# Top-k attention and MLP on one core: conversion by an integer add, division after the values product, loads in order of need

## The chip, the cores and the metric

The kernel runs on one core of a Trainium2 chip. Its engines work side by side, each on its own queue of instructions: TensorE (in the profile PE for matmuls and PEld for the loading of their stationary operands), VectorE (DVE), ScalarE (ACT), GpSimd (POOL) and SyncE (SP), which issues all DMAs here. The metric is the device time of one execution in microseconds (us); lower is better.

## The reference

Two blocks follow each other. The first is attention that keeps only the 32 largest scores of each row:

```python
scores = scale * np.matmul(q, k.transpose(0, 1, 3, 2))          # 8 x 8 heads, 576 x 576
kth = np.partition(scores, -top_k, axis=-1)[..., -top_k:-top_k + 1]
scores = np.where(scores >= kth, scores, -1000000000.0)
attn = np.exp(scores - np.max(scores, axis=-1, keepdims=True))
attn = attn / (np.sum(attn, axis=-1, keepdims=True) + 1e-09)
attn_out = np.matmul(attn, v)                                   # (8, 8, 576, 64)
```

The second is an MLP on its output, taken as 4608 tokens of 512 features:

```python
h = x @ w_in                                                    # 4608 x 2048
g = np.where(h >= 1, h, np.where(h <= -1, 0.0, (h + 1) ** 2 / 4))
out = g @ w_out                                                 # 4608 x 512
```

q, k and v are fp32. `w_in` and `w_out` come as 64-bit floats, so the kernel reads each number as two 32-bit words (`lo`, `hi`) and makes an fp32 number of them itself. Numbers that are nearly zero are set to zero (the comparison of `size` with 1.125 * 2^-15).

## The kernel before

Attention is cut into 144 steps. A step is one tile of 128 query rows for a pair of heads (`t < NT`), or, for the last 64 rows of a sequence, a tail tile that serves two pairs (`t == NT`). `steps` lists them in order: batch by batch, within a batch tile by tile, within a tile pair by pair.

Each step goes through these functions. `scores` (L209) multiplies queries and keys on TensorE into four PSUM tiles `sp` and copies them to `s` on ScalarE (L224). `weights` (L229) finds the 32nd largest value on VectorE: it takes the larger of each two scores (`more`, L238), then four rounds of `max` and three of `match_replace` (L244, L251), then the smaller ones (`less`, L256) to see whether a pair hid a large second score. ScalarE forms `exp` (L248) once GpSimd has the negated maximum (L246). VectorE masks `e` and sums it (L271), takes the reciprocal `rz` of the sum (L277), and GpSimd multiplies `e` by it (L279). `transpose_w` (L283) turns `e` on TensorE in eight transposes plus one for the 64 left-over columns of both heads, and ScalarE copies them to `wT` and `wTt` (L291, L294). `values` (L297) multiplies them by v into a PSUM tile `po`, which ScalarE copies to `xT` (L318, L320), the input of the MLP.

The MLP of a chunk of one or two tiles is a list of work items (`mlp`, L329): sixteen `hidden` (TensorE into `ph`, two activations on ScalarE, three operations on GpSimd, L343 to L345), then `final` items, two of the sixteen slices of `w_out` each, into `py`; the last copies `y` and stores it.

The loop of L445 sets the order. Iteration m issues, on TensorE, values(m-2), scores(m+1), some MLP items, transpose_w(m-1), the transposes of later queries and keys, more MLP items; on VectorE, weights(m). The order on TensorE and VectorE is that of the program (`manual_schedule`, L411); ScalarE, GpSimd and the DMA queue are ordered by a scheduler. How many MLP items an iteration takes is decided when the program is built: `share` is what is left divided by the iterations left, an item is taken when its cost is covered and the weights that it needs are `converted`, and unspent credit is capped at 8. Where a chunk is used up before the next is ready, iterations hold no MLP item. This happens around the iterations 14 to 16, 25, 26, 61, 62, 96 to 98, 106, 124 and 134 to 136.

All PSUM tiles of attention share one tag of four buffers (`tag="a", bufs=4`), handed out in turn: in iteration m `po` takes one, the four `sp` of scores(m+1) the next four, so the fourth needs the buffer of `po` back.

The weights are converted in 64 pieces of 128 x 256 numbers (`weight_piece`, L78). A piece takes three operations on VectorE (L85, L86, L90), two on ScalarE (L92, L97), two on GpSimd (L93, L94), and, one piece later, the mask on VectorE (L99). `convert` is called four times ahead of step 0 and six times in each `weights`, from the callback `between` (four rounds, after the masking, after the reciprocal), so the pieces are done in step 9.

After all steps the largest `excess` is turned into a flag (L475 to L483). If the shortcut with pairs was not enough, the whole is run again without it (L485).

Of the kernel before, what the change touches and what calls it, by code (L numbers as in the profile page):

```python
# [22 lines left out]
def kernel(  # L23
# [10 lines left out]
    nc = tc.nc  # L34
# [25 lines left out]
    nc.gpsimd.memset(minus, -1.0)  # L60
    w_in = const.tile([P, NK, DFF], F32, name="w_in")
# [16 lines left out]
    def weight_piece(pool, dst, src):  # L78
        raw = pool.tile([P, 2 * WC], U32, name="raw", bufs=2)
        nc.sync.dma_start(out=raw, in_=src.bitcast(U32))  # L80
        words = raw.rearrange("p (n t) -> p n t", t=2)
        lo, hi = words[:, :, 0], words[:, :, 1]

        top = pool.tile([P, WC], U32, name="top", bufs=2)
        nc.vector.tensor_scalar(top, hi, 3, 0x3FFFFFFF, ALU.logical_shift_left, ALU.bitwise_and)  # L85
        nc.vector.scalar_tensor_tensor(out=top, in0=hi, scalar=0xC0000000, in1=top,  # L86
                                       op0=ALU.bitwise_and, op1=ALU.bitwise_or)

        unit = pool.tile([P, WC], U32, name="unit", bufs=2)
        nc.vector.tensor_scalar(unit, top, 0xFF800000, None, ALU.bitwise_and)  # L90
        low = pool.tile([P, WC], F32, name="low", bufs=2)
        nc.scalar.activation(low, lo, AF.Copy, scale=2.0 ** -52)  # L92
        nc.gpsimd.tensor_tensor(out=low, in0=low, in1=unit.bitcast(F32), op=ALU.mult)  # L93
        nc.gpsimd.tensor_tensor(out=low, in0=low, in1=top.bitcast(F32), op=ALU.add)  # L94

        size = pool.tile([P, WC], F32, name="size", bufs=2)
        nc.scalar.activation(size, hi.bitcast(F32), AF.Abs)  # L97
        yield
        nc.vector.scalar_tensor_tensor(out=dst, in0=size, scalar=1.125 * 2.0 ** -15, in1=low,  # L99
                                       op0=ALU.is_ge, op1=ALU.mult)  # L100

    def weight_pieces(pool):

        pieces = [(w_in[:, kk, c:c + WC], moe_w_in[kk * P:(kk + 1) * P, c:c + WC])
                  for c in range(0, DFF, WC) for kk in range(NK)]
        pieces += [(w_out[:, f, c:c + WC], moe_w_out[f * P:(f + 1) * P, c:c + WC])
                   for f in range(NF) for c in range(0, DM, WC)]
        before = None
        for dst, src in pieces:
            piece = weight_piece(pool, dst, src)  # L110
# [11 lines left out]
    def run(ctx, paired):  # L122
# [47 lines left out]
        def keys_of(b):  # L170

            kT = stage.tile([P, NHP, S], F32, name="kT")
            v_in, v_tl = load_values(b)
            k_tl = stage.tile([TL, H, D], F32, name="k_tl", bufs=1)
            nc.sync.dma_start(out=k_tl, in_=k[b, :, SM:S, :].rearrange("h p d -> p h d"))
            for hp in range(NHP):
                k_in = stage.tile([P, NT, 2, D], F32, name="k_in")
                for j in range(2):
                    nc.sync.dma_start(out=k_in[:, :, j, :], in_=whole(k, b)[:, 2 * hp + j])
                pt = ps.tile([P, NT, P], F32, name="pk", tag="a", bufs=4)  # L180
# [13 lines left out]
                yield dict(kT=kT, v=v_in, v_tl=v_tl)  # L194
# [34 lines left out]
        def weights(st, between):  # L229
# [48 lines left out]
            for i in range(2):  # L278
                nc.gpsimd.tensor_scalar(e[:, i, :], e[:, i, :], rz[:, i:i + 1], 1.0, ALU.mult, ALU.mult)  # L279
# [3 lines left out]
        def transpose_w(st):  # L283
            w = st["e"]
            st["wT"] = wT = att.tile([P, 2, NT, P], F32, name="wT", bufs=1)
            st["wTt"] = wTt = att.tile([P, P], F32, name="wTt", bufs=1)
# [5 lines left out]
            pt = ps.tile([P, P], F32, name="pwt", tag="a", bufs=4)  # L292
            nc.tensor.transpose(pt, w.rearrange("p i n -> p (i n)")[:, SM:SM + P], ident)
            nc.scalar.copy(wTt, pt)  # L294


        def values(st):  # L297
            t, hp, v_in, v_tl = st["t"], st["hp"], st["keys"]["v"], st["keys"]["v_tl"]
            wT, wTt = st["wT"], st["wTt"]
            po = ps.tile([P, P], F32, name="po", tag="a", bufs=4)  # L300
            if t < NT:
                for c in range(NT + 1):
                    for j in range(2):
                        h = 2 * hp + j
                        nc.tensor.matmul(po[j * D:(j + 1) * D], v_in[:, h, c, :] if c < NT else v_tl[0][:, h, :],  # L305
                                         wT[:, j, c, :] if c < NT else wTt, start=(c == 0), stop=(c == NT))
            else:
                for i in range(2):
                    cols = slice(i * TL, (i + 1) * TL)
                    for c in range(NT + 1):  # L310
                        for j in range(2):
                            h = 2 * (hp + i) + j
                            nc.tensor.matmul(po[j * D:(j + 1) * D, cols], v_in[:, h, c, :] if c < NT else v_tl[1][:, h, :],
                                             wT[:, i, c, j * TL:(j + 1) * TL] if c < NT else wTt[:, j * TL:(j + 1) * TL],
# [106 lines left out]
        for got in keys_of(0):  # L421
            keys[0] = got
# [92 lines left out]
```

## Time and profile before

| | |
|---|---|
| median of 3 runs | 1918.03 us (1916.92 to 1918.96) |
| the profiled execution | 1915.05 us, span 1913.0 us |
| TensorE busy (PE) | 1679.1 us, 88% of the span |
| VectorE busy (DVE) | 1625.4 us, 85% |
| GpSimd busy (POOL) | 1028.8 us, 54% |
| ScalarE busy (ACT) | 977.1 us, 51% |
| mean granted TensorE clock | 0.942 |
| the chain that ended last | PE 53%, DVE 22%, POOL 13%, ACT 6%, issue 5%, DMA 1% |

The span runs from the first instruction to the last. "L244 x1152" is line 244 of the kernel, executed 1152 times; the tiles are written out<-in. In an answer on waits, "PE pw L290 <- POOL e L279" says that TensorE stood idle before the instruction of line 290 that writes `pw` until GpSimd finished the instruction of line 279 that writes `e`. In a timeline each row has its start and its length in us, the engine, the line, the operation, and in brackets the idle time ahead of it. An average over the whole span hides that the stages have different limits, so the stages have to be read one by one.

### The profile page before, as it was taken

To read this page: it belongs to the slowest core of one execution; us is meant where nothing else is said; L and a number is where in the kernel's file an instruction comes from. 1 tells how busy PE (TensorE), PEld (TensorE's weight loads), DVE (VectorE), ACT (ScalarE), POOL (GpSimd) and SP (SyncE) were. 2 spreads that over 40 slices of the span, in tenths; PEclk is the share of its full clock that TensorE was granted. 3 is DMA by queue.
4 is the path that set the end of the run, shared out by engine and by line. 5 is a ranking of instruction groups with operands and counts; after the bars stand their busy time and mean duration, and the time that the engine had idled before them with its cause. 6 is when DMAs were issued, how large, how long until landed. Compare 5 with 4: busy or idle time off the path is not lost.

```text
span 1913.0 us, 32251 instructions
## 1 busy us (share of the span) xinstructions
PE 1679.1 (88%) x10129; PEld 1160.1 (61%) x10129; DVE 1625.4 (85%) x5011; ACT 977.1 (51%) x2429; POOL 1028.8 (54%) x1772
## 2 busy tenths in 40 slices
PE   2346478898999999998999999998999999998998
PEld 1234255656676685767575776666676667666565
DVE  5998989999999799999898898989987879879640
ACT  4345455546455564655454655555455555445432
POOL 3567572725454672818283674637274554553553
PEclk8667679899999999999999999999999999998999
DMA  6222210011010000110010000110010000000000
GB/s 173 80 78 77 77 28 17 26 30 24 9 40 20 23 18 23 32 36 12 16 38 23 21 12 24 40 27 12 23 31 25 11 12 11 10 12 7 6 7 14
DMA packets 107445, 57.75 MB, mean 30 GB/s; under 512 B 86272, under 2 KB 94464, under 8 KB 107264
## 3 DMA queue, kind: packets, MB, share of 16 engines
q1 hardware_dynamic: 107264, 55.59, 10.6%
q8 instruction: 82, 1.34, 0.3%
q14 instruction: 99, 0.81, 0.1%
HBM read 46.14 MB, written 9.44 MB: 29 GB/s over the span
## 4 chain that ended last, share of the span: by engine, by line
PE 53%; DVE 22%; POOL 13%; ACT 6%; issue 5%; DMA 1%; POOLq 0%; SPq 0%; DVEq 0%; ACTq 0%
PE py L353 24%; PE ph L336 11%; PE sp L221 6%; DVE tops L244 6%; PE po L305 5%; DVE more L251 5%; PE pw L290 4%; POOL g L345 4%; POOL r L344 3%; POOL e L279 2%; POOL r L343 2%; DVE e L271 2%; DVE more L238 2%; DVE seconds L259 2%; DVE less L256 1%
## 5 line engine op out<-in xcount | busy, mean ns | idle before, releaser
L353 PE MATMUL py<-w_out,g 128*128 128x512 f32 x1152 | 534.7, 607 | 41.7 <-DVE w_out L99 37.1
L336 PE MATMUL ph<-xT,w_in 128*128 128x256 f32 (+1 forms) x2816 | 553.3, 353 | 3.9 <-ACT g L342 2.8
L336 PEld LDWEIGHTS ph<-xT,w_in 128*128 128x128 f32 x2816 | 466.4, 197 | 83.0 <-issue 29.4
L244 DVE MAX8 tops<-more 128x8 f32<-128x288 f32 x1152 | 468.5, 448 | 5.0
L353 PEld LDWEIGHTS py<-w_out,g 128*128 128x128 f32 x1152 | 209.2, 191 | 286.4 <-issue 219.8
L251 DVE MATCH_REPLACE8 more<-tops,more 128x288 f32<-128x288 f32 x864 | 375.9, 443 | 0.0
L279 POOL TENSOR_SCALAR e<-e,rz 128x576 f32<-128x576 f32 x288 | 242.4, 850 | 130.9 <-DVE rz L277 104.9
L340 ACT ACTIVATE r<-ph,half 128x256 f32<-128x256 f32 (+1 forms) x352 | 153.9, 437 | 264.2 <-POOL g L345 135.2
L264 POOL TENSOR_TENSOR excess<-seconds,kth 128x2 f32<-128x2 f32 x144 | 39.2, 273 | 417.3 <-DVE kth L263 416.4
L271 DVE SCALAR_TENSOR_TENSOR e<-s,kth,e 128x576 f32<-128x576 f32 x288 | 242.4, 875 | 23.1 <-ACT e L248 6.6
L345 POOL TENSOR_TENSOR g<-r,g 128x256 f32<-128x256 f32 (+1 forms) x352 | 246.7, 701 | 24.0
L291 ACT COPY wT<-pw 128x512 f32<-128x512 f32 x288 | 155.5, 594 | 202.3 <-PE pw L290 202.3
L290 PE MATMUL pw<-ident,e 128*128 128x128 f32 x1152 | 161.5, 284 | 110.6 <-POOL e L279 105.9
L248 ACT ACTIVATE e<-s,nmax 128x576 f32<-128x576 f32 x288 | 213.1, 786 | 75.2 <-POOL nmax L246 74.4
L238 DVE TENSOR_TENSOR more<-s 128x576 f32<-128x576 f32 x144 | 130.4, 905 | 139.0 <-ACT s L224 138.6
L344 POOL TENSOR_TENSOR r<-r 128x256 f32<-128x256 f32 (+1 forms) x352 | 230.4, 655 | 26.1
L290 PEld LDWEIGHTS pw<-ident,e 128*128 128x128 f32 x1152 | 138.0, 146 | 162.5 <-POOL e L279 118.2
L221 PE MATMUL sp<-kT,qT 64*128 64x288 f32 x1024 | 196.5, 442 | 34.7 <-ACT xT L318 26.4
L224 ACT ACTIVATE s<-sp 128x288 f32<-128x288 f32 x576 | 197.9, 417 | 40.7 <-PE sp L221 36.8
L343 POOL TENSOR_SCALAR r<-r 128x256 f32<-128x256 f32 (+1 forms) x352 | 155.4, 441 | 93.5 <-ACT r L340 93.2
L305 PEld LDWEIGHTS po<-wT,v_in 128*64 128x64 f32 x2048 | 118.0, 140 | 74.8 <-issue 40.0
L221 PEld LDWEIGHTS sp<-kT,qT 64*128 64x128 f32 x1024 | 109.1, 189 | 84.6 <-ACT xT L318 39.4
(61 smaller groups left out, 1592.7 us busy)
## 6 DMA issues: line engine op xcount, KB each, us to landing
q_in<-in_q_dram SPq DMA_DIRECT2D x32, 256.0 KB, 3.0
v_in<-in_v_dram SPq DMA_DIRECT2D x8, 1024.0 KB, 5.8
k_in<-in_k_dram SPq DMA_DIRECT2D x64, 128.0 KB, 3.0
raw<-in_moe_w_in_dram SPq DMA_DIRECT2D x32, 256.0 KB, 2.7
raw<-in_moe_w_out_dram SPq DMA_DIRECT2D x32, 256.0 KB, 2.8
out_dram<-y SPq DMA_DIRECT2D x32, 256.0 KB, 2.3
v_tail<-in_v_dram SPq DMA_DIRECT2D x16, 64.0 KB, 2.5
k_tl<-in_k_dram SPq DMA_DIRECT2D x8, 128.0 KB, 3.2
```

Of the source, the lines that this page charges most:

```text
L221: nc.tensor.matmul(o[:, a0 - c0:a1 - c0], qT[d, g, :], kT[d, g, k0:k0 + a1 - a0], start=True, stop=True)
L244: nc.vector.max(out=tops[:, i, r:r + 8], in_=src[:, i, :])
L248: nc.scalar.activation(e[:, i, :], s[:, i, :], AF.Exp, bias=nmax[:, i:i + 1])
L251: nc.vector.match_replace(out=rest[:, i, :], in_to_replace=tops[:, i, r:r + 8], in_values=src[:, i, :], imm_value=LOWEST)
L271: nc.vector.scalar_tensor_tensor(out=e[:, i, :], in0=s[:, i, :], scalar=last[:, i:i + 1], in1=e[:, i, :], op0=ALU.is_ge, op1=ALU.mult, acc ...
L279: nc.gpsimd.tensor_scalar(e[:, i, :], e[:, i, :], rz[:, i:i + 1], 1.0, ALU.mult, ALU.mult)
L290: nc.tensor.transpose(pt[:, c, :], w[:, i, main(i)][:, c * P:(c + 1) * P], ident)
L305: nc.tensor.matmul(po[j * D:(j + 1) * D], v_in[:, h, c, :] if c < NT else v_tl[0][:, h, :], wT[:, j, c, :] if c < NT else wTt, start=(c == ...
L336: nc.tensor.matmul(ph, w_in[:, kk, f * P:(f + 1) * P], xT[:, kk, 0:cw], start=(kk == 0), stop=(kk == NK - 1))
L344: nc.gpsimd.tensor_tensor(out=r, in0=r, in1=r, op=ALU.mult)
L345: nc.gpsimd.tensor_tensor(out=g[:, 0:cw], in0=r, in1=g[:, 0:cw], op=ALU.add)
L353: nc.tensor.matmul(py, gs[f][:, i * P:(i + 1) * P], w_out[:, f, :], start=(f == 0), stop=(f == NF - 1))
```

## The change

Five things change.

1. Loads. `keys_of` issues the keys of the first head pair first, then the 64-row remainder, and v after the second pair. For batch 0 only the first pair is prepared before step 0; the others follow after the first eight conversions. `raw` has three buffers where it had two.
2. Conversion. The low word becomes a number between 2 and 2 + 2^-19 (`units`). Its bits, added as an integer on GpSimd to the shifted high word, round the mantissa and mend the exponent in one operation. VectorE shifts (one operation) and later puts the sign in (one). For `w_in` the mask moves to GpSimd (a comparison and a product); for `w_out` it stays on VectorE.
3. Division. GpSimd no longer scales `e`. `rz` is spread by a ScalarE copy to `rzw`, transposed on TensorE behind the left-over columns (one transpose, two in a tail step), copied with `wTt`, and `divide` multiplies `po` by it on VectorE when it writes `xT` (two instructions in a tail step). `divide(m-2)` is run from the first `between` of weights(m), that is after the first round of step m.
4. MLP share. In iterations 0 to 11 the share is at least 52, and eight pieces are converted ahead of step 0.
5. Flag. `judge` runs in the last iteration with attention, right after weights(143), instead of after everything. `y` has one buffer where it had two.

The core of the diff:

```diff
-    def weight_piece(pool, dst, src):
-        raw = pool.tile([P, 2 * WC], U32, name="raw", bufs=2)
+    def weight_piece(pool, dst, src, mask_engine):
+        raw = pool.tile([P, 2 * WC], U32, name="raw", bufs=3)
...
-        nc.vector.tensor_scalar(top, hi, 3, 0x3FFFFFFF, ALU.logical_shift_left, ALU.bitwise_and)
-        nc.vector.scalar_tensor_tensor(out=top, in0=hi, scalar=0xC0000000, in1=top,
-                                       op0=ALU.bitwise_and, op1=ALU.bitwise_or)
...
-        nc.vector.tensor_scalar(unit, top, 0xFF800000, None, ALU.bitwise_and)
...
-        nc.gpsimd.tensor_tensor(out=low, in0=low, in1=unit.bitcast(F32), op=ALU.mult)
-        nc.gpsimd.tensor_tensor(out=low, in0=low, in1=top.bitcast(F32), op=ALU.add)
...
+        nc.scalar.activation(units, lo, AF.Identity, bias=two, scale=2.0 ** -51)
...
+        nc.vector.tensor_scalar(bits, hi, 3, None, ALU.logical_shift_left)
+        nc.gpsimd.tensor_tensor(out=bits.bitcast(I32), in0=bits.bitcast(I32), in1=units.bitcast(I32), op=ALU.add)
+        if mask_engine is nc.gpsimd:
+            nc.gpsimd.tensor_scalar(size, size, 1.125 * 2.0 ** -15, 1.0, ALU.is_ge, ALU.mult)
         yield
-        nc.vector.scalar_tensor_tensor(out=dst, in0=size, scalar=1.125 * 2.0 ** -15, in1=low,
-                                       op0=ALU.is_ge, op1=ALU.mult)
+        nc.vector.scalar_tensor_tensor(out=bits, in0=hi, scalar=0x80000000, in1=bits,
+                                       op0=ALU.bitwise_and, op1=ALU.bitwise_or)
+        if mask_engine is nc.gpsimd:
+            nc.gpsimd.tensor_tensor(out=dst, in0=size, in1=bits.bitcast(F32), op=ALU.mult)
+        else:
+            nc.vector.scalar_tensor_tensor(out=dst, in0=size, scalar=1.125 * 2.0 ** -15, in1=bits.bitcast(F32),
+                                           op0=ALU.is_ge, op1=ALU.mult)
...
-            for i in range(2):
-                nc.gpsimd.tensor_scalar(e[:, i, :], e[:, i, :], rz[:, i:i + 1], 1.0, ALU.mult, ALU.mult)
+            if st["t"] < NT:
+                st["rzw"] = rzw = att.tile([P, 2, D], F32, name="rzw")
+                nc.scalar.copy(rzw, rz.unsqueeze(2).broadcast_to([P, 2, D]))
...
+            if st["t"] < NT:
+                nc.tensor.transpose(pt[:, 1], rzw.rearrange("p i d -> p (i d)"), ident)
+                nc.scalar.copy(wTt[:, 0:2], pt[:, 0:2])
...
+        def divide(st):
...
-                nc.scalar.copy(xT[:, hp, col:col + P], po)
+                nc.vector.tensor_tensor(out=xT[:, hp, col:col + P], in0=po, in1=wTt[:, 1], op=ALU.mult)
...
-        for _ in range(4):
+        for _ in range(8 if paired else 0):
             convert()
...
+            def between():
+                if todo:
+                    todo.pop()()
+                convert()
+
             if 2 <= m:
                 values(state[m - 2])
+                todo.append(partial(divide, state[m - 2]))
+            share = max((total - spent) / (n + 2 - m), 52 if paired and m < 12 else 0)
...
+                weights(state[m], between)
+            elif todo:
+                todo.pop()()
...
+            if m == n - 1 and paired:
+                judge(ps, att)
...
+    def judge(ps, att):
+        worst = att.tile([P, 8], F32, name="worst", bufs=1)
+        nc.vector.max(out=worst, in_=excess)
+        pt = ps.tile([1, P], F32, name="pworst", tag="a", bufs=4)
+        nc.tensor.transpose(pt, worst[:, 0:1], ident)
```

## The prediction

> **What bounds the kernel now.** I read the page's engine shares first, then busy time by stage, then the waits of PE and DVE, then the timeline around one step. Stages (columns: stretch, its length, busy us and count of PE, PEld, DVE, ACT, POOL, then the granted clock, DMA share, GB/s):
>
> ```profile
> 0.00:30.60 30.60, 11.18 (x48) 8.09 (x48) 8.37 (x20) 14.50 (x34) 8.66 (x21) 1.00 0.77 202
> 30.60:252.20 221.60, 88.76 (x478) 59.56 (x478) 208.22 (x569) 93.81 (x244) 140.60 (x207) 0.66 0.28 79
> 252.20:333.20 81.00, 73.29 (x514) 53.71 (x515) 72.16 (x233) 45.65 (x119) 37.05 (x78) 0.94 0.08 21
> 333.20:1750.00 1416.80, 1360.30 (x8304) 938.76 (x8303) 1261.86 (x3960) 760.05 (x1865) 757.64 (x1295) 0.98 0.08 22
> 1750.00:1873.70 123.70, 115.20 (x631) 79.40 (x630) 73.87 (x233) 52.46 (x135) 66.98 (x126) 0.97 0.02 7
> ```
>
> Loads set the first 30.6 us (202 GB/s). Steps 0 to 9, in which the weights are converted, are VectorE's (208 of 222 us). From step 17 (333 us) TensorE is the bound: 57 us idle in 1417. So VectorE's time counts early, and any instruction or wait of TensorE counts late.
>
> Waits of TensorE and VectorE (engine, line, what it waited for: total us, times, longest):
>
> ```profile
> PE pw L290 <- POOL e L279: 105.9, 14, 25.2
> PE py L353 <- DVE w_out L99: 37.1, 10, 6.9
> PE sp L221 <- ACT xT L318: 26.4, 24, 5.2
> DVE more L238 <- ACT s L224: 138.6, 68, 8.5
> ```
>
> The first two are nearly all early (95.6 and 37.1 us before 300 us): there TensorE waits for VectorE's pace, not for GpSimd itself. Late, VectorE waits for scores: it is ahead. How far ahead decides my forecast. Step 61 begins at 839.21; its first round of top-k ends at 841.67:
>
> ```profile
> 839.21 0.76 DVE L238 TENSOR_TENSOR more<-s 128x576 f32<-128x576 f32 x1
> 841.23 0.44 DVE L251 MATCH_REPLACE8 more<-tops,more 128x288 f32<-128x288 f32 x1
> 850.55 0.77 DVE L238 TENSOR_TENSOR more<-s 128x576 f32<-128x576 f32 x1 [0.78 <-ACT s L224]
> 860.92 0.74 DVE L238 TENSOR_TENSOR more<-s 128x576 f32<-128x576 f32 x1
> ```
>
> ScalarE copies the values product of step 59 only at 848.95, 7.3 us later; the next copies follow after 4.3, 4.6 and 12.2 us:
>
> ```profile
> 848.95 0.27 ACT L318 COPY xT<-po 128x128 f32<-128x128 f32 x1
> 853.27 0.25 ACT L318 COPY xT<-po 128x128 f32<-128x128 f32 x1
> 857.83 0.27 ACT L318 COPY xT<-po 128x128 f32<-128x128 f32 x1 [0.17 <-PE po L305]
> 870.07 0.27 ACT L318 COPY xT<-po 128x128 f32<-128x128 f32 x1
> ```
>
> Where no MLP work is pending, a TensorE iteration takes 4.5 us and TensorE runs through the steps that VectorE did in advance. A step costs VectorE 10.4 us (850.55 to 860.92).
>
> **The change part by part.** The profiled execution took 1915.05 us (span 1913.0 and 2 around it), 3 under the median of 1918.03. I sum against it and add the 3.
>
> *Loads.* The first `more` waits for the loads queued before it. Section 6 gives their sizes: q and k of one head pair, the small q and k loads, nine weight pieces of 256 KB, v of 1 MB and its tails make 5.0 MB now, against 5.7 MB before; at 202 GB/s that is 25 against 28 us, so the first step begins near 27.5: -3 (bounds -6 to +2, since eight pieces must now pass GpSimd first, at 0.84 + 0.44 + 0.79 = 2.1 us each by L94, L343, L93: 16.5 us from a first landing near 9). SP also passes the next batch's k behind transposes, as before; `raw` has one buffer more to cover it.
>
> *Conversion.* Before: L85, L86, L90, L99 cost VectorE 0.377 + 0.557 + 0.367 + 0.449 = 1.75 us per piece, 60 pieces inside steps 0 to 9: 105 us. After: a shift (as L85) and a merge (as L86), 0.93, and for w_out also the mask, 1.38; eight w_in pieces are ahead of step 0, so 24 x 0.93 + 32 x 1.38 = 66.6. Gain 38; eight divisions (0.33 each, below) take 2.6: -36. These prices depend on GpSimd: at 24.09 L85 took 0.29 alone, at 25.62 beside L93 0.77. Clean prices (0.29 + 0.43) give -50, a quarter more -20.
>
> The Trainium skill (GPSIMD Engine Reference, Engine selection) advises against elementwise two-input work on GpSimd, about twice as slow as VectorE. Moving the mask product costs 32 x (0.79 - 0.45) = 11 us of engine time by the rows, and if GpSimd were the bound the sum would be 11 worse. But GpSimd is idle for 81 of 222 us in that stage, so I take 0. The same page calls an all-int32 add there exact and gives it no rate; I use L94's 0.84 (bounds 0.7 to twice that).
>
> *Order of MLP work early.* A share of 52 pulls one-tile MLP work into steps 5, 6, 9 and 10: up to 60 units, fifteen `hidden` at 1.16 us (eight matmuls at 1889.82) plus 5 of attention, 22 us against a 19 us VectorE step. TensorE also waits in step 7 for w_out pieces finished only at the end of that step. I count 4 + 3.5 + 11 + 7 = 26 us of such waits; before, gaps in steps 0 to 16 made 22. +4 (bounds -8 to +12).
>
> *Division.* GpSimd's two L279 leave each step, 1.7 us off a path that late carries nothing. Added: on ScalarE a copy of `rz` and a wider `wTt` in place of `xT`, about +0.15 a step; on TensorE one transpose per step, two in a tail step: 160 x 0.14 (161.5/1152), about 19 after step 17, where all of it counts. Alone a transpose takes 0.28 (L293), so 19 to 38: +19, since it stands beside another. On VectorE a 128-column product from PSUM: L260 does 16 columns in 0.22, L256 576 in 0.81, a line through both gives 0.34; L482 read 128 columns of PSUM in 0.29. I take 0.33.
>
> The waits matter more. VectorE's `divide(m-2)` stands after the first round of step m and must wait for the values product that TensorE makes at the head of iteration m. All that VectorE did in advance, 6 to 9 us, is gone; behind it queue the rest of step m and all later steps. And `po` holds its PSUM buffer until then: the fourth score tile, four allocations later, waits for VectorE instead of ScalarE. So both engines meet once per step and every iteration costs the longer of the two. Of the intervals between `xT` copies of steps 17 to 135, seventeen are under 9.9 us and sum to 112; at 10.3 + 0.33 each they take 180: +68. Before, TensorE paid 25 of this back idle in the intervals after them (gaps of 0.3 to 4.6 us, the longest in the 19.2 us after step 62): net +43 (bounds 20 to 60). Iterations of 10.5 or more cost nothing, as the score tile is needed 1.2 us after the product.
>
> Gone are TensorE's waits for the `xT` copy: -24 (18.0 + 5.7 after 356 us). New on ScalarE: in 50 steps its order puts the `rz` copy, which needs the end of step m, ahead of the last `wT` copy of step m-1, and `exp` of step m+1 ahead of later MLP evictions. In MLP-heavy iterations VectorE needs 11.3 (L238 beside GpSimd's MLP), so values start near 11 and end near 12.5 where TensorE had 11.7 to 12.4. I take 0.35 in each of the 50: +18 (bounds 0 to 45).
>
> *Clock.* The row: at 880.30 to 883.70, after waits of 1.7 and 1.9 us, the granted clock is 0.50; over the whole late stage 0.98. I take +4 for twelve new waits near 6 us (0 to 15). The Trainium skill (TensorE: Matmul & The Clock Gate, Part 1) halves the clock after an idle window of about 3.4 us; with one window lost per wait, 12 x 1.7 = 20 would stand in place of 4, but the iterations between waits hold only 4.5 us of work in 10.6, which hides most.
>
> *Flag.* The chain at the end goes: the last copy ends at 1905.34, TensorE's transpose 1905.39, flag 1906.18; now TensorE's branch follows its last matmul at 1904.7: -1.5. But the transpose of `worst` now stands on TensorE right behind values(141), and needs all of step 143 on VectorE, which itself divides 141 first: 8.0 us (10.9 in that step of before) + 0.46 + 0.3 while TensorE has nothing ahead of it in order: +10 (8 to 13). Before, TensorE had no gap there. One `y` buffer for two costs nothing: 16 matmuls of 0.43 us lie between two copies, an output lands in 2.3.
>
> **Sum.** -3 - 36 + 4 + 19 + 43 - 24 + 18 + 4 - 1.5 + 10 = +33.5 on 1915, 1948.5; against the median 1951.
>
> **The rivals.** (1) Faster: the early gain decides. If the meeting point does not bind, because VectorE's lead is lost only where it was not used, the +43, +18 and +4 vanish: 1918 - 31.5 = 1886; with half of the 65, 1919. It decides from under 31 us of late waits. For it: 1262 of 1417 us busy on VectorE leaves it room. Against it: the seventeen short intervals. 0.20. (2) ScalarE's and GpSimd's order becomes the bound of MLP-heavy iterations (some 64): 1 us in each of 64 instead of 18 in all: 1997. For it: POOL spends 0.49 + 0.77 + 0.81 per `hidden`, up to five in 11.5 us, and now waits for step ends. 0.18. (3) The conversion does not do what it says: the integer add runs at half speed and GpSimd, 6 x 2.9 = 17.4 us a step, keeps pace with VectorE's 16; half of the 36 goes: 1969. 0.12. (4) Terms cancel, within 0.2% (4 us, about what this kernel's runs can tell): 0.04.
>
> **How the numbers follow.** The forecast has 0.46, with its own range 1930 to 1968. The 0.20 of rival 1 reaches to 1886; a low end of 1893 leaves about 0.12 below, 1988 about 0.08 above. Faster 0.20, same 0.04, slower 0.76.
>
> **What would show it.** Right: the stage to step 17 shorter by some 30 us; VectorE waiting at the division for `po` in most late steps, in total over 300 us, with `more` hardly waiting; score tiles waiting for VectorE's `xT`; a gap near 10 us before the transpose of `worst`; no interval between divisions under 10 us. Wrong: VectorE's waits at the division end early without TensorE waiting at `sp`, or the first stage shrinks by 60.

## The result, and the profile after

The changed kernel takes 1946.48 us (median, 1944.48 to 1947.55) against 1918.49 us before (1916.92 to 1919.89). The ratio is 1.0145, with a 95% interval of 1.0127 to 1.0162: slower by some 28 us, in the range and 4.5 us under the forecast of 1951. The profiled execution took 1944.48 us, span 1942.7. Its busy time by stage, cut where steps 0, 17 and 136 begin (columns: stretch, its length, busy us and count of PE, PEld, DVE, ACT, POOL, granted clock, DMA share, GB/s):

```profile
0.00:31.50 31.50, 7.17 (x28) 4.53 (x28) 8.23 (x18) 14.20 (x31) 21.33 (x36) 1.00 0.66 174
31.50:321.00 289.50, 177.55 (x1018) 123.24 (x1018) 236.28 (x721) 149.93 (x365) 147.25 (x236) 0.82 0.24 69
321.00:1766.90 1445.90, 1371.30 (x8413) 952.01 (x8414) 1285.94 (x4064) 781.51 (x1857) 608.59 (x1054) 0.98 0.08 21
1766.90:1942.70 175.80, 150.96 (x832) 104.53 (x830) 86.89 (x278) 68.55 (x177) 73.55 (x160) 0.95 0.02 7
```

The kernel before, cut at the same steps:

```profile
0.00:30.60 30.60, 11.18 (x48) 8.09 (x48) 8.37 (x20) 14.50 (x34) 8.66 (x21) 1.00 0.77 202
30.60:333.20 302.60, 162.05 (x992) 113.26 (x993) 280.38 (x800) 139.45 (x363) 177.66 (x284) 0.74 0.22 64
333.20:1739.80 1406.60, 1352.36 (x8265) 933.02 (x8263) 1251.96 (x3929) 756.01 (x1855) 755.49 (x1291) 0.99 0.08 22
1739.80:1913.00 173.20, 153.47 (x826) 105.74 (x826) 84.67 (x268) 67.10 (x177) 87.04 (x178) 0.94 0.02 7
```

Read stage by stage, the change costs 0.9 us at the start, gains 13.1 in steps 0 to 16, loses 39.3 in steps 17 to 135 and 2.6 at the end. In the third stage TensorE is busy 18.9 us longer and idle 20.4 us longer (74.6 against 54.2).

The waits of TensorE and VectorE (engine, line, what it waited for: total us, times, longest):

```profile
PE ph L362 <- DVE xT L340: 48.9, 10, 12.2
PE pw L302 <- DVE e L278: 43.1, 11, 8.9
...
PE pworst L521 <- DVE worst L519: 8.9, 1, 8.9
```

```profile
DVE xT L340 <- PE po L324: 158.3, 68, 11.8
DVE bits L93 <- POOL w_in L101: 27.2, 19, 3.5
...
DVE bits L98 <- POOL bits L94: 10.5, 5, 3.7
```

VectorE no longer waits at `more` (138.6 us before); it waits at the division, and TensorE now waits for that division. Step 61 and the steps behind it show the pace, in the timeline of VectorE:

```profile
837.55 0.74 DVE L245 TENSOR_TENSOR more<-s 128x576 f32<-128x576 f32 x1
840.89 0.29 DVE L340 TENSOR_TENSOR xT<-po,wTt 128x128 f32<-128x128 f32 x1 [0.90 <-PE po L324]
...
851.39 0.28 DVE L340 TENSOR_TENSOR xT<-po,wTt 128x128 f32<-128x128 f32 x1
...
861.89 0.28 DVE L340 TENSOR_TENSOR xT<-po,wTt 128x128 f32<-128x128 f32 x1
```

and, in the same place, of TensorE:

```profile
850.38 1.09 PE L324 MATMUL po<-wT,v_in 128*64 128x128 f32 x16
851.30 0.39 PE L324 MATMUL po<-wTt,v_tail 128*64 128x128 f32 x4
...
862.23 5.60 PE L362 MATMUL ph<-xT,w_in 128*128 128x256 f32 x18 [6.38 <-DVE xT L340]
```

The divisions follow after 10.5 and 10.5 us. Before, the copies of `xT` in this place followed after 4.3 and 4.6 us. TensorE has finished the product of step 61 at 851.7, but the next chunk's MLP cannot begin until VectorE has come to that step's division at 861.89, and TensorE stands idle for 6.38 us. Over the whole stage, 17 intervals between copies were under 9.9 us before; now the shortest of all is 10.5.

The first stages, by the groups of GpSimd (line, tiles, shapes, count, busy us, mean ns of one, idle before), show the other surprise:

```profile
L94 POOL TENSOR_TENSOR bits<-bits,units 128x256 int32<-128x256 int32 x64 | 48.4, 757 | 55.1 <-DVE bits L93 33.0 <-ACT units L87 15.3 <-ACT size L90 3.8
L369 POOL TENSOR_SCALAR r<-r 128x128 f32<-128x128 f32 x128 | 42.7, 333 | 47.3 <-ACT r L366 47.3
L96 POOL TENSOR_SCALAR size<-size 128x256 f32<-128x256 f32 x32 | 36.4, 1142 | 3.7 <-ACT size L90 3.7
```

The integer add takes 0.757 us, no longer than the floating-point add of before (0.836). The comparison takes 1.142, not the 0.44 that the prediction used; GpSimd needs about 2.8 us for a piece of `w_in`, and VectorE waits for it.

### The profile page after: what moved, and what is told of

Read it like the earlier page. It is cut to its first block, busy times and chain, and to the rows that moved or that the text cites. A ratio compares the mean times of both kernels' runs of the same rounds, so it can differ in the third digit from the quotient of the medians.

```text
span 1942.7 us, 31981 instructions
## 1 busy us (share of the span) xinstructions
PE 1707.0 (88%) x10289; PEld 1184.3 (61%) x10289; DVE 1617.3 (83%) x5075; ACT 1014.2 (52%) x2429; POOL 850.7 (44%) x1485
## 4 chain that ended last, share of the span: by engine, by line
PE 58%; DVE 27%; POOL 7%; issue 4%; ACT 2%; DMA 0%; SPq 0%; DVEq 0%; POOLq 0%; ACTq 0%
PE py L379 22%; PE ph L362 18%; DVE tops L251 8%; PE po L324 6%; DVE more L258 6%; PE sp L228 6%; PE pw L302 4%; DVE e L278 3%; DVE seconds L266 2%; DVE more L245 2%; DVE less L263 2%; POOL size L96 1%; POOL bits L94 1%; POOL g L371 1%; POOL r L370 1%
## 5 line engine op out<-in xcount | busy, mean ns | idle before, releaser
L271 POOL TENSOR_TENSOR excess<-seconds,kth 128x2 f32<-128x2 f32 x144 | 97.9, 680 | 567.8 <-DVE kth L270 567.4
L371 POOL TENSOR_TENSOR g<-r,g 128x256 f32<-128x256 f32 (+1 forms) x352 | 242.0, 688 | 27.8 <-POOL r L370 1.6
L278 DVE SCALAR_TENSOR_TENSOR e<-s,kth,e 128x576 f32<-128x576 f32 x288 | 236.7, 858 | 4.7
L370 POOL TENSOR_TENSOR r<-r 128x256 f32<-128x256 f32 (+1 forms) x352 | 221.6, 630 | 27.2
L369 POOL TENSOR_SCALAR r<-r 128x256 f32<-128x256 f32 (+1 forms) x352 | 161.3, 458 | 161.7 <-ACT r L366 161.6
L228 PE MATMUL sp<-kT,qT 64*128 64x288 f32 x1024 | 205.5, 449 | 24.7 <-ACT s L231 6.5
L340 DVE TENSOR_TENSOR xT<-po,wTt 128x128 f32<-128x128 f32 x128 | 36.9, 288 | 181.9 <-PE po L324 158.3
L228 PEld LDWEIGHTS sp<-kT,qT 64*128 64x128 f32 x1024 | 113.3, 190 | 78.5 <-issue 23.5
L324 PE MATMUL po<-wT,v_in 128*64 128x128 f32 x2048 | 152.1, 286 | 3.6 <-ACT wT L303 2.9
```

Source lines behind the costliest of these rows:

```text
L228: nc.tensor.matmul(o[:, a0 - c0:a1 - c0], qT[d, g, :], kT[d, g, k0:k0 + a1 - a0], start=True, stop=True)
L278: nc.vector.scalar_tensor_tensor(out=e[:, i, :], in0=s[:, i, :], scalar=last[:, i:i + 1], in1=e[:, i, :], op0=ALU.is_ge, op1=ALU.mult, acc ...
L370: nc.gpsimd.tensor_tensor(out=r, in0=r, in1=r, op=ALU.mult)
L371: nc.gpsimd.tensor_tensor(out=g[:, 0:cw], in0=r, in1=g[:, 0:cw], op=ALU.add)
```

## The experiments

Theory A: in the late stage VectorE used to run ahead of TensorE and to leave it a store of finished steps; the division makes the two engines meet once per step, and what is lost is that store (with, as the theory had it, the clock that TensorE loses in its new waits, and the extra transposes). Its rivals: the changed order of the MLP work (B), the transposes and copies themselves (C, T), ScalarE's order (S). Theory D: GpSimd paces the start. All kernels are the changed kernel with the edit shown, but three that build on another run, as their expectations say; `...` marks what is left out.

### Without the division

```diff
+            for i in range(2):
+                nc.gpsimd.tensor_scalar(e[:, i, :], e[:, i, :], rz[:, i:i + 1], 1.0, ALU.mult, ALU.mult)
-            rzw ... its copy and its transposes
-            nc.vector.tensor_tensor(out=xT[:, hp, col:col + P], in0=po, in1=wTt[:, 1], op=ALU.mult)
+            nc.scalar.copy(xT[:, hp, col:col + P], po)
```

> The division part alone is undone: the scaling of e is back on GpSimd, ScalarE copies po to xT, no transposes of rzw; loads, conversion, share and the early flag stay. Theory A (VectorE's meeting with the values product plus the extra transposes make the late loss): steps 17 to 135 go back from 1443 to about 1405 us, VectorE waits at `more` for scores again, and the kernel takes 1944 - 38 = about 1906 us; the scaling on GpSimd (two by 0.84 us a step) can take back up to 8 us early, so 1904 to 1914. Theory B (the late loss comes from the changed order of the MLP work, which a faster conversion and the share of 52 bring, not from the division): steps 17 to 135 stay near 1440 and the time over 1935.

Measured: 1898.35 us (1895.38 to 1899.45), ratio to before 0.9889 (0.9873 to 0.9906). The division alone costs 48 us, and the rest of the change is a gain of 21. By stage:

```profile
31.30:316.10 284.80, 175.99 (x1012) 121.45 (x1013) 234.78 (x706) 146.92 (x367) 170.83 (x270) 0.75 0.23 70
316.10:1722.30 1406.20, 1349.86 (x8265) 931.08 (x8263) 1252.79 (x3929) 754.86 (x1855) 755.10 (x1291) 0.99 0.08 22
1722.30:1893.50 171.20, 153.25 (x826) 105.84 (x826) 84.76 (x268) 66.99 (x177) 86.64 (x178) 0.94 0.02 8
```

Steps 17 to 135 are back at 1406.2 us, as before the change (1406.6), and the 17 short intervals are back. Theory B falls: the MLP order and the share stayed, and the loss went. The time is some 6 us under the expected range of 1904 to 1914, because the other two stages are shorter too: step 17 begins at 316.1 instead of 321.0, and the last stage takes 171.2 instead of 175.8.

### The product with 1/sums on GpSimd instead of VectorE

```diff
-                nc.vector.tensor_tensor(out=xT[:, hp, col:col + P], in0=po, in1=wTt[:, 1], op=ALU.mult)
+                nc.scalar.copy(xT[:, hp, col:col + P], po)
+                nc.gpsimd.tensor_tensor(out=xT[:, hp, col:col + P], in0=xT[:, hp, col:col + P], in1=wTt[:, 1], op=ALU.mult)
```

> The division stays behind the values product, with all its transposes and copies of rz, but off VectorE: ScalarE copies po to xT and GpSimd multiplies xT in place. So VectorE no longer waits for TensorE inside a step. Theory A (the meeting of VectorE and TensorE once per step is most of the late loss): no interval-floor of 10.5 us is left, `more` waits for scores again, steps 17 to 135 take about 1405 + 19 = 1424 us, the kernel about 1926. Theory C (the transposes and ScalarE's copies of rz are the loss, the meeting costs nothing): steps 17 to 135 stay within 5 us of 1443 and the kernel within 5 us of 1946.

Measured: 1960.72 us (1958.41 to 1966.05), slower than the changed kernel, and outside both expectations. The short intervals are back (17 of them), `more` waits for scores again (215.1 us), and yet steps 17 to 135 take 1478.5 us. The waits of TensorE and the timeline of ScalarE say where a new wait stands:

```profile
PE sp L228 <- ACT xT L340: 63.8, 40, 4.9
```

```profile
882.88 0.30 ACT L288 COPY rzw<-rz 128x128 f32<-128x128 f32 x1 [2.28 <-DVE rz L284]
883.08 0.47 ACT L369 ACTIVATE g<-ph,minus 128x256 f32<-128x256 f32 x1
883.45 0.26 ACT L340 COPY xT<-po 128x128 f32<-128x128 f32 x1
```

```profile
883.76 1.32 PE L228 MATMUL sp<-kT,qT 64*128 64x288 f32 x2 [1.62 <-ACT xT L340]
```

ScalarE's copy of `rz` needs the end of VectorE's step (it stands idle for 2.28 us before 882.88), and behind it queue the copy of `po` and an eviction of `ph`. TensorE's fourth score tile needs the buffer of `po`. So the engines meet again, this time through ScalarE's order; the short intervals alone do not tell the time. Not all of the loss is waiting: of the 32.6 us by which the third stage is longer than in the changed kernel, TensorE is idle for 7.3 and busy for 25.3 (1396.6 against 1371.3), at a granted clock of 0.97 against 0.98. The run does not answer its question; it names a second culprit, which the runs with `rz` on GpSimd below take up.

### Without the transposes

```diff
-                nc.tensor.transpose(pt[:, 1], rzw.rearrange("p i d -> p (i d)"), ident)
-                nc.scalar.copy(wTt[:, 0:2], pt[:, 0:2])
+            nc.scalar.copy(wTt[:, 0], pt[:, 0])
-                nc.vector.tensor_tensor(out=xT[:, hp, col:col + P], in0=po, in1=wTt[:, 1], op=ALU.mult)
+                nc.vector.tensor_tensor(out=xT[:, hp, col:col + P], in0=po, in1=ones, op=ALU.mult)
```

> Left out: the transposes of rzw; the product with 1/sums is a product with ones, so the output is undivided. VectorE still makes its product from po in the same place. The prediction's step (19 us, each of 160 transposes at 0.14 us on the path) expects steps 17 to 135 at 1424 and the kernel at about 1926. Theory A in its sharper form (iterations held at 10.5 us by the meeting hide the transpose, only the others pay): a gain of about half, 8 to 12 us, 1934 to 1938. If neither counts: within 3 us of 1946.

Measured: 1935.62 us (1934.6 to 1936.63), 10.9 under the changed kernel, the number of theory A in its sharper form. The third stage:

```profile
316.80:1757.60 1440.80, 1361.92 (x8277) 940.60 (x8278) 1281.79 (x4063) 764.14 (x1857) 609.93 (x1054) 0.97 0.08 21
```

TensorE is busy for 9.4 us less than in the changed kernel with 136 matmuls fewer. That is not yet the price of the transposes, because the granted clock differs: 0.97 here, 0.98 in the changed kernel, 0.99 before. In the clock records of the traces every value in this stage is 1.0 or 0.5, so what the clock cost can be estimated as half of the time that TensorE worked at 0.5 (three rows near the end show 7 matmuls in 2.8 us at 0.50 and 15 in the next 2.8 us at 0.96). TensorE worked so for 52.9 us here, for 31.5 in the changed kernel and for 34.8 before: a cost of 26.4, 15.8 and 17.4 us. So this kernel, busy for 9.6 us more than before (1352.36) with the same matmuls but for twelve records, pays 9.0 of them to the clock; and against the changed kernel, at equal clock, it would be busy for some 20 us less and not 9.4, 0.15 for each transpose.

The third-stage gain is only 5.1 us of length, as the idle time rises to 78.9. The rest of the difference lies in the first 320 us, which vary from kernel to kernel here (below). So not all of the 10.9 can be put down to the transposes, and that the number fell into the expected range is in part luck.

### The mask of w_in on VectorE

```diff
-        pieces = [(w_in[:, kk, c:c + WC], moe_w_in[kk * P:(kk + 1) * P, c:c + WC], nc.gpsimd)
+        pieces = [(w_in[:, kk, c:c + WC], moe_w_in[kk * P:(kk + 1) * P, c:c + WC], nc.vector)
```

> Only the mask of the w_in pieces goes from GpSimd (comparison 1.14 us and product 0.85 us a piece) to VectorE (one instruction of 0.45 us), as w_out has it. Theory D (GpSimd paces the start and steps 0 to 3): the first `more` comes about 3 us earlier than 31.5, steps 0 to 3 take about 19 instead of 20.4 us, step 17 begins near 311 instead of 321, and the kernel takes about 1936. Rival (VectorE has no room for 32 by 0.45 = 14 us more, or TensorE's early MLP work sets steps 4 to 16): step 17 begins at 318 or later and the time is within 4 us of 1946 or above.

Measured: 1941.98 us (1939.56 to 1948.06), ratio to before 1.0119 (1.0096 to 1.0141). Step 0 begins at 28.2 instead of 31.5 us and step 17 at 313.3 instead of 321.0: theory D, with steps 0 to 3 at 20.4, 18.5, 18.7, 18.7 us instead of 22.0, 20.6, 19.9, 19.1. Of the 7.7 us some 4 are left in the median, and the intervals of the two kernels overlap: in the profiled execution 7 us are lost again in steps 17 to 135 (1452.9 us), whose code is the same. They go with the clock: TensorE is busy for 7.2 us longer there and worked at half clock for 47.2 us instead of 31.5, which costs 7.8. Why it was granted less the runs do not say.

### The reciprocal written wide by VectorE

```diff
-            nc.vector.reciprocal(rz, z)
-                nc.scalar.copy(rzw, rz.unsqueeze(2).broadcast_to([P, 2, D]))
+                nc.vector.reciprocal(rzw, z.unsqueeze(2).broadcast_to([P, 2, D]))
```

> After, with one thing changed: VectorE writes the reciprocals straight into the wide tile rzw (one instruction, about 0.1 us longer), and ScalarE's copy of rz, which waits for the end of a step ahead of other work in ScalarE's order, is gone. Theory S (the prediction's step of 0.35 us in each of 50 steps: ScalarE's order holds the late stage): 1946 - 18 = about 1928 us. Theory A (the meeting of VectorE and TensorE and the transposes are all of the loss): the time stays within 5 us of 1946, or rises to 1954, since the longer instruction stands on VectorE in every iteration held at 10.5 us.

Measured: 1991.74 us (1990.91 to 1992.17), outside all expectations, for a reason that the groups of VectorE give:

```profile
L285 DVE RECIPROCAL rzw<-z 128x128 f32<-128x128 f32 x128 | 122.0, 953 | 4.4
L337 DVE TENSOR_TENSOR xT<-po,wTt 128x128 f32<-128x128 f32 x128 | 36.8, 287 | 135.4 <-PE po L321 102.7 <-ACT g L365 23.6 <-ACT e L255 7.6
L288 DVE RECIPROCAL rzwt<-z 128x256 f32<-128x256 f32 x16 | 28.0, 1753 | 1.2
```

A reciprocal of 128 columns takes 0.953 us, where one of two columns took 0.166 and a product of 128 columns takes 0.287. So this run lengthens VectorE's step by 0.79 us, and it measures what such a step costs: the shortest interval between divisions rises from 10.5 to 11.2 us, and steps 17 to 135 from 1445.9 to 1483.7, 38 us, while VectorE is busy there for 81 us more (1367.0 against 1285.9). Under half of the added work is on the path, and part of the 38 is clock: TensorE is busy for 22 us more, at 0.97 against 0.98. The run says nothing for or against ScalarE's order.

### The division one step later, and po in a place of its own

Three kernels gave `po` the unused half of the PSUM banks of `ph`, as one tile with it: one of them also divides a step later, one does only this, and one is meant as a better kernel.

```diff
+        both = ps.tile([P, 3, 512], F32, name="both")
-            st["po"] = po = ps.tile([P, P], F32, name="po", tag="a", bufs=4)
+            st["po"] = po = both[:, st["m"] % 3, CW:CW + P]
-                ph = ps.tile([P, CW], F32, name="ph", tag="ph", bufs=3)[:, 0:cw]
+                ph = both[:, next(turn) % 3, 0:cw]
```

```diff
-                if todo:
-                    todo.pop()()
+                if len(todo) > 1:
+                    divide(todo.popleft())
```

> After, with the division on VectorE one step later: the product of step m-2 is divided after the first round of step m+1, not of step m. For this po has a place of its own (the unused half of the banks of ph) and a chunk's MLP may begin one iteration later. ScalarE's copy of rz, the transposes and VectorE's instruction stay. Theory A (the meeting takes VectorE's lead): VectorE may now be a step ahead again, its waits at the division (157 us after 330 us) shrink below 60, steps 17 to 135 take 1400 to 1425 instead of 1446 us, the kernel 1900 to 1925. Theory S (ScalarE's order, not the meeting): 1938 to 1948.

> After, with only the place of po changed as in the run with the later division: it no longer takes one of the four buffers that the score tiles use. The division stays where it is. Theory A: the meeting at the division stays, with its floor of 10.5 us per iteration; only TensorE's waits of score tiles for VectorE's xT go (8.4 us after 330 us): 1936 to 1946. If the score tile's wait for the division was what held both engines together: below 1925.

> The run without the division part, with the mask of all weight pieces on VectorE and po in a place of its own. TensorE's waits of score tiles for ScalarE's copy of po (27.2 + 5.7 us after 330 us) go, and about 4 us of the start: 1898 - 33 - 4 = 1861 if nothing takes their place; 1880 if half of them turn into waits for weights or copies further on; 1894 if all do.

Measured: 2400.94, 2377.4 and 2174.54 us. All three are far slower, and show the same new wait, read from the waits of TensorE in the second:

```profile
PE both L365 <- ACT g L371: 247.2, 224, 3.3
```

The matmuls of a `hidden` wait 224 times for ScalarE's eviction `g` (232 and 226 times in the other two; 15 waits, 13.4 us, in the changed kernel). The reading that fits: as one tile the three banks no longer alternate, and a matmul into one is held until the reader of another is done. No run separates this from the sharing of a bank by `po` and `ph`. The runs say nothing of the meeting, and the division on VectorE one step later stays unmeasured.

### GpSimd copies rz: the two suspects apart

Two kernels take ScalarE's copy of `rz` away without lengthening VectorE, one with the division on VectorE, the other with the product on GpSimd.

```diff
-                nc.scalar.copy(rzw, rz.unsqueeze(2).broadcast_to([P, 2, D]))
+                nc.gpsimd.tensor_copy(rzw, rz.unsqueeze(2).broadcast_to([P, 2, D]))
```

> After, with GpSimd copying rz in place of ScalarE; VectorE's division stays where it is. Theory A (VectorE's meeting alone holds the late stage): within 6 us of 1946, with no interval between divisions under 10.5 us. Theory S (ScalarE's order is a cost of its own, 18 us in the prediction): about 1928.

> The run that divides on GpSimd, with GpSimd copying rz as well, so ScalarE's order has no copy that waits for the end of a step (in that run it stood between the score copies of the next step). The division stays behind the values product and all its transposes stay. Theory A (what counts is VectorE's lead, whether VectorE's own wait or ScalarE's order takes it away; the transposes cost what is left): VectorE waits for scores again, steps 17 to 135 take the 1406 us of the run without the division plus up to 19 for 160 transposes, the kernel 1905 to 1920. Theory T (moving the division costs in TensorE time and GpSimd latency whatever the waits): above 1935.

Measured, as a square of times in us:

| | ScalarE copies rz | GpSimd copies rz |
|---|---|---|
| VectorE divides from po | 1946.48 (the changed kernel) | 1951.87 (1948.28 to 1952.26) |
| ScalarE copies po, GpSimd multiplies | 1960.72 | 1888.76 (1887.98 to 1890.47) |

Taking away either wait alone gains nothing; taking away both gains 58 us. (The 5 us between the two kernels of the first row go with the clock again: in the third stage TensorE worked at half clock for 47.0 us in the second and for 31.5 in the first.) Each of the two ties TensorE to the end or the middle of VectorE's step, and one is enough. The kernel with neither is 16 us under the range that theory A gave it, and beats the kernel before: ratio 0.9839 (0.9823 to 0.9855), with the division still behind the values product and all 160 transposes in place. Its stages and the copies of `xT` around step 61:

```profile
316.60:1722.00 1405.40, 1354.15 (x8387) 938.60 (x8388) 1248.34 (x3928) 769.88 (x1852) 680.09 (x1304) 0.99 0.08 22
1722.00:1887.10 165.10, 150.51 (x831) 102.95 (x829) 84.90 (x268) 67.62 (x177) 82.12 (x178) 0.98 0.02 8
```

```profile
830.82 0.27 ACT L340 COPY xT<-po 128x128 f32<-128x128 f32 x1
835.10 0.25 ACT L340 COPY xT<-po 128x128 f32<-128x128 f32 x1
839.59 0.27 ACT L340 COPY xT<-po 128x128 f32<-128x128 f32 x1
851.94 0.27 ACT L340 COPY xT<-po 128x128 f32<-128x128 f32 x1
```

The intervals are 4.3, 4.5 and 12.4 us, as before the change. Against the run without the division TensorE is busy for 4.3 us more with 122 matmuls more, and this third stage is no longer: 1405.4 against 1406.2. So moving the division costs nothing here. That does not make the transposes free: the clock cost 4.3 us less here (10.7 against 15.0), ten `hidden` matmuls fewer fall into the stage, and GpSimd no longer scales `e`. Theory T falls, and theory S as a separate term falls with the other run of the pair. The last stage, 165.1 us, is 6.1 shorter than without the division. There, in the run without the division as before the change, TensorE's `pw` waited 3.1 us for GpSimd's scaling of `e` and `sp` 6.6 for the copy of `po`; now `sp` waits 3.5 and `pw` not at all.

### Without the division, the mask on VectorE

> The run without the division part, with the mask of all weight pieces on VectorE. If the two gains add (48 and 4 us): 1894. If VectorE's 14 us more take back what GpSimd's relief gives, since VectorE is ahead in neither: 1898 to 1904.

The edits are those of the first and the fourth run together. Measured: 1887.97 us (1886.7 to 1891.31), ratio 0.9839 (0.9823 to 0.9856), better than the sum of the two gains and under all that was expected. Step 17 begins at 306.3 instead of 316.1: without the waits of the late stage, the whole 10 us arrive at the end. Here the relief of GpSimd is plain. This kernel and the one with product and copy on GpSimd are equal within their spread, and both beat the kernel before by some 31 us. The two edits were not tried together.

### The flag at the end

```diff
-            if m == n - 1 and paired:
-                judge(ps, att)
+    ... worst, pworst, top8 and flag after run(inner, True), as before
```

> After, with the flag formed at the end as in before. The wait of 8.9 us before the transpose of `worst` goes, and the chain at the end, 1 to 2.5 us, comes back. If the wait is on the path: 1946 - 9 + 2 = 1939. If TensorE makes up for it in the iterations behind: 1946 to 1949.

Measured: 1936.98 us (1933.71 to 1942.46), 9.5 under the changed kernel. The last stage:

```profile
1764.30:1931.90 167.60, 149.75 (x832) 103.97 (x831) 86.51 (x278) 68.56 (x177) 73.78 (x160) 0.96 0.02 8
```

167.6 us against 175.8: the wait of 8.9 us ahead of the transpose of `worst` was on the path. With VectorE ahead of TensorE the early flag is free: in the run without the division, and in the one with neither wait, TensorE has no wait of this kind, and VectorE waits 0.7 and 0.5 us for the transpose.

## Why the prediction was right, and where its terms were off

Forecast 1951, measured 1946.5; the sum for the profiled execution was 1948.5, measured 1944.48. The direction and the mechanism were right: the meeting of VectorE and TensorE. That the sum came so close is luck: the gain up to step 17 was 23 us smaller than predicted, the loss of the late stage 21 us smaller and that of the end 6.

| stage | predicted, us | measured, us |
|---|---|---|
| to the first `more` | -3 | +0.9 |
| steps 0 to 16: conversion, MLP order | -36 + 4 | -13.1 |
| steps 17 to 135: lockstep, transposes, `xT` waits, ScalarE's order, clock | 43 + 19 - 24 + 18 + 4 = +60 | +39.3 |
| step 136 to the end: flag | +8.5 | +2.6 |

**Loads and conversion.** The largest mistake that a run shows is GpSimd's comparison: taken at 0.44 from the row of a minimum and maximum (L343), it takes 1.142. With it "GpSimd is idle for 81 of 222 us, so I take 0" failed: busy 68.7 of the 81.5 us of steps 0 to 3, GpSimd sets their pace. That was the place of rival 3, but by the comparison and not by the integer add, which is not slow. With the mask on VectorE the first `more` comes at 28.2 and 28.7 us, near the 27.5 predicted; with it on GpSimd it comes between 28.9 and 31.5. With that mask alone changed, steps 0 to 16 take 285.1 us instead of 289.5. The division costs here too, which the prediction left out: without it and with that mask they take 277.6, a gain of 25 us, and the start gains 2, against 35 predicted. What is missing still is in TensorE's early MLP work: in that kernel steps 4 and 5 take 21.8 and 25.2 us beside 18.6 of their neighbours (24.2, 25.3 and, in step 6, 22.6 beside 21.5 before), and steps 10 and 11 take 18.4 and 16.1 where before they took 13.9 and 14.6. That is 9.8 + 6.0 - 7.6, some 8 us, where the term had +4; the share of 52 was not tried alone. VectorE's own prices held: 24 pieces by 0.346 + 0.446 and 32 by 0.346 + 0.446 + 0.687 make 66, as predicted, though the mask of `w_out` alone takes 0.687 and not 0.45.

The Trainium skill (GPSIMD Engine Reference, Engine selection) calls one-input operations on GpSimd roughly line-rate and two-input ones about twice as slow as on VectorE. The second agrees with the nearest rows here: the mask product takes 0.853 on GpSimd, VectorE's two-input merge (L98) of the same shape 0.446. The first does not: the one-input comparison of the same shape took 1.142 on GpSimd, more than the two-input product, and the measurement decides.

**The lockstep.** "Every iteration costs the longer of the two" was right: no interval under 10.5 us is left, the 17 short ones come back when both waits go. Of the third stage's +39.3, TensorE's idle time is 20.4 where 43 - 24 + 18 = 37 was predicted. The new waits of TensorE in that stage stand less at the score tiles, where the prediction put them, than at the start of a chunk's MLP:

```profile
PE ph L362 <- DVE xT L340: 30.5, 8, 6.4
PE pw L302 <- DVE e L278: 12.1, 5, 5.0
```

There was no wait of the first kind before, and 3.9 us at the same transposes for GpSimd's scaling of `e`. VectorE's waits at the division, predicted at over 300 us, are 168 in 76 waits. That sign missed, and it did not fit the prediction's own sum: 1262 us of VectorE's work before and 0.33 for each of 119 divisions leave some 175 idle in a stage of 1417 + 60 us. Taking away single causes, as the terms suggest, misleads: the +18 for ScalarE's order does not exist beside the meeting (1951.87 without it), yet ScalarE's order alone holds the kernel at 1960.72 where VectorE's meeting is gone. In the sum it had to be counted once, as part of one condition, not as a term of its own. The waits that were to go went in part: in the third stage score tiles waited 23.7 us for `xT` before and 8.4 now, so the term of -24 was worth -15.

**Transposes.** 0.14 each was taken, 19 us after step 17. The timeline of TensorE in the changed kernel agrees roughly:

```profile
836.56 0.27 PE L305 MATMUL pwt<-ident,e 128*128 128x128 f32 x1
836.67 0.27 PE L308 MATMUL pwt<-ident,rzw 128*128 128x128 f32 x1
836.77 0.60 PE L208 MATMUL pq<-ident,q_in 128*128 128x128 f32 x4
```

A transpose of `rzw` starts 0.11 us after the one before it, and the next matmul 0.10 us after that. For the 135 of the third stage that makes an estimate of 15 us; the comparison with the run without them, at equal clock, gives 20. How much of it is on the path is not shown: leaving them out gains 5.1 us of the stage at a lower clock, and the kernel without both waits has them in a stage no longer than the run without the division.

**Clock.** +4 was taken for new waits near 6 us, twelve of them. TensorE stands idle for over 3 us six times in the third stage, twice before. The clock cost no more than before by the estimate above, 15.8 us against 17.4, so the +4 does not show in the changed kernel, and TensorE's longer busy time of 18.9 us is mostly transposes. Two kernels with the same late code on TensorE pay 23.6 and 23.5, some 6 more than before. What one such wait does the clock records do show. The wait of 6.38 us shown above leaves this behind, in three windows of the changed kernel (columns as in the stages; the granted clock is the third number from the end):

```profile
855.90:862.20 6.30, 0.00 (x0) 0.00 (x0) 5.99 (x21) 0.96 (x2) 1.01 (x2) 0.70 0.00 0
862.20:865.00 2.80, 2.77 (x7) 2.23 (x8) 2.80 (x12) 1.62 (x4) 0.88 (x2) 0.50 0.00 0
865.00:867.80 2.80, 2.80 (x15) 2.44 (x14) 2.66 (x7) 0.84 (x2) 1.88 (x4) 0.96 0.00 0
```

TensorE's first 2.8 us of work after the wait run at a clock of 0.50. The Trainium skill (TensorE: Matmul & The Clock Gate, Part 1) says that an idle window of about 3.4 us halves the clock and that it takes a busy window to bring it back, which agrees with these rows; of the 20 us worked out by it in the prediction the third stage shows nothing. With the clock's cost between 15.8 and 23.6 us for the same late code on TensorE, a difference of up to some 8 us between two kernels can be the clock's alone.

**Flag.** The price of the wait (+10 in the prediction, less 1.5 for the chain) was right: undoing it gains 9.5 us, 8.2 of them in the last stage. What the step left out is a gain of the division in that stage: with the flag at the end it takes 167.6 us, before 173.2, which fits that no scaling of `e` stands between the last masking and the last transposes.

**Rivals.** Rival 1 (the early gain decides) would have been the outcome without the meeting, and the runs without it end at 1888 to 1898, near its 1886. Rival 2 (the order of ScalarE and GpSimd bounds the MLP-heavy iterations) is not what holds the changed kernel, but its mechanism is what the run with the product on GpSimd found.

**Open.** Why TensorE worked at half clock for 78.3 us in the third stage of the run with the product on GpSimd, 47 more than in the changed kernel: by the estimate that costs 23 us, more than the 14 by which the run is slower. Open too are how much of the transposes' time is on the path, and the division on VectorE a step later.

## What to carry to other kernels

An instruction that consumes another engine's product, put early into a long in-order sequence, makes the two engines meet there once per round, and what it costs is the store of finished work that one of them had: look for the short intervals in the trace of before, since those can be lost. When several in-order queues can tie the same two engines, undoing one of them may show nothing; test them in pairs before a cause is dropped. Before two kernels' busy times are subtracted, their granted clocks have to be compared. A price for an operation is good for that operation only: a comparison is not a minimum, and a reciprocal is not a product.

## What the runs showed of the hardware that was not expected

- GpSimd, one input of 128x256: comparison and product by a constant 1142 ns, minimum and maximum 530 ns. Integer add of the same shape 757 ns, floating-point add 836 ns.
- VectorE: reciprocal of 128x128 953 ns, of 128x256 1753 ns, of 128x2 166 ns, where a product of 128x128 takes 287 ns. So a sum is better inverted first and spread afterwards (the copy to 128x128 took 297 ns on ScalarE, and 440 and 578 ns on GpSimd in two runs). The Trainium skill (VectorE: DVE Perf Modes, First, the fixed hardware budget) names an iterative division with a repeat count of 8 for the reciprocal; the rows agree in direction, with a slope of 6.3 ns a column between the two wide ones.
- A 128-column fp32 transpose issued right behind another starts 0.11 us after it, while one takes 0.28 us from start to end.
- In the clock records of the third stage the granted clock of TensorE is 1.0 or 0.5 and nothing between (other values in rows are averages). The changed kernel and the one with the mask on VectorE, whose late code on TensorE is the same, worked for 31.5 and 47.2 us at half clock.
